# A matrix-memory LSTM with a token and channel mixer: the k q products of two chunks in one run, the transposes in slots 2 and 6

## The chip, the cores and the metric

The kernel runs on one core of a Trainium2 chip. The metric is device time in microseconds (us) of one execution; three executions of the kernel before were timed, at 432.81 us in the median. TensorE is called PE in the profile (PEld for its weight loads), VectorE DVE, ScalarE ACT, GpSimd POOL and SyncE SP; SPq is SyncE's queue, which issues nearly all of the loads here.

## The reference

Four batches of 8 heads, 768 tokens, head width 40. First comes a recurrence with exponential gates, then a token mixer and a channel mixer over the 320 columns of all heads.

```python
for t in range(S):                                   # S = 768
    m_new = np.maximum(f[t] + m, i[t])
    f_stab, i_stab = np.exp(f[t] + m - m_new), np.exp(i[t] - m_new)
    C = f_stab * C + i_stab * outer(v[t], k[t])      # 40 x 40 for each head
    n = f_stab * n + i_stab * k[t]
    y[t] = sigmoid(o[t]) * (C @ q[t]) / max(abs(n @ q[t]), 1)
h  = relu(y.T @ w_tok1) @ w_tok2                     # 768 -> 256 -> 768, over tokens
u  = y + h.T
out = u + relu(u @ w_ch1) @ w_ch2                    # 320 -> 1536 -> 320
```

## The kernel before

**Attention.** Each batch is cut into 6 chunks of 128 tokens; a unit `u` is the pair (batch, chunk), both counted from 0 in the code. In this document the batches are called first to fourth, and chunks go by their number in the code, 0 to 5. In a chunk the recurrence becomes matrix products. `st_s` (L302) multiplies k by q for all 8 heads: 16 matmuls, two at a time on different rows of the array (heads 0 to 3 lie on partitions 0 to 39, heads 4 to 7 on 64 to 103 of the tile `raw`, padded to 64 rows each), and writes two PSUM banks, the tiles `ps_sc`. `st_p` (L312) has VectorE multiply these banks by the decay mask `dd`, one instruction for each bank. `st_state` (L357) adds the chunk to the state: the three products `pu` of k and v, then five VectorE instructions that build the new state `Cn`; for the second batch it also starts the output bank `po` with q times the state before the chunk (L367). `st_pv` (L411) adds the product of masked scores and v to that output. The third and fourth batches (`three(u)`) use `st_pv3` (L388) in its place: the scores are split into three bf16 parts by VectorE (`prep_p2`, `prep_p3`), the product is made from these, q times the state stands behind it (L403), and `st_state` is called at its end.

**Order.** All engines run in program order, as the code is written. `att(b)` (L513) is a generator with five steps a chunk: (1) `st_s` with `st_p`, and loads for the chunk after next; (2) `st_state` or `prep_p3`; (3) the mask's exponentials for the next chunk; (4) `st_pv`, and what follows from its output (`st_hs`, `st_x`); (5) the rest of the next chunk's preparation. The loop at the end (L993) walks 18 slots a batch. A slot holds `gemm1` of one piece of the channel mixer (16 matmuls, L756), then what `more` lists for the slot, then some steps of the next batch's attention, then `gemm2` of the piece before (12 matmuls, L675, in two halves). So the second batch's attention runs inside the first batch's slots 11 to 17 (`STEPS0`, L928), the third's inside the second's slots, and the fourth's inside the third's (`STEPS`, L929). The fourth batch's slots have no attention beside them.

**The slots of the later batches.** `phase_b` (L699) is the second product of the token mixer for one chunk, `phase_t` (L726) transposes the result (three matmuls against the identity, one ScalarE copy and two or three VectorE instructions) so that `gemm1` can read it. In the second to fourth batch the dictionary `more` (L991) puts `phase_b` of chunk 4 into slot 1, `phase_t` of chunk 2 into slot 2, `phase_t` of chunk 3 into slot 4, `phase_b` of chunk 5 into slot 5, and `phase_t` of chunks 4 and 5 into slot 9.

**Banks and loads.** Four PSUM pools of two banks each: `ps_h`, `ps_acc`, `ps_s` (tag "s": the scores, and what is passed `ss`) and `ps_m` (tag "m": outputs, states). A new tile of a pool takes the bank of the tile two before it, and its first writer waits until that tile's last reader is through. The tile `raw` has three buffers, used in turn; its two halves are loaded for the chunk after next, the first in step 1 and the second in step 3 (L228). All loads go out on one queue in the order of the program: for each chunk of the second batch the mask rows `dd` (512 KB), the two halves of `raw` (160 KB each), `q3t` and `pq` (180 KB each) and `kvt` (324 KB), and the gate `sig` (480 KB) twice a batch.

Of the kernel before, what the change touches and what calls it, by code (L numbers as in the profile page):

```python
# [7 lines left out]
F32 = mybir.dt.float32  # L8
# [12 lines left out]
E1 = D + 1  # L21
# [13 lines left out]
def kernel(ctx: ExitStack, tc: tile.TileContext, gates, qk, q3, kv, og,  # L35
# [8 lines left out]
    ps_s = ctx.enter_context(tc.tile_pool(name="ps_s", bufs=2, space=PSUM))  # L44
    ps_m = ctx.enter_context(tc.tile_pool(name="ps_m", bufs=2, space=PSUM))
# [6 lines left out]
    def load_sig(b, i):  # L52
        t = ap.tile([128, NC // 2, DM], F32, tag="sig", name="sig", bufs=3)
        nc.sync.dma_start(out=t, in_=og[b].rearrange("(c p) e -> p c e", p=128)[:, 3 * i:3 * i + 3, :])
        sig[(b, i)] = t
# [111 lines left out]
    def top(x):  # L167
        return x.bitcast(BF16).rearrange("... (t i) -> ... t i", i=2)[..., 1]
# [47 lines left out]
    def sigmoid(b, r=range(2), part=slice(0, 3)):  # L216
        for i in r:
            t = sig[(b, i)][:, part]
            nc.scalar.activation(t, t, AF.Sigmoid)
# [25 lines left out]
    def load_q3(u):  # L245
        b, c = u
        if c > 0:
            load_pq(u, load_q3t(u))
# [53 lines left out]
    def st_s(u, mult=True, mid=iter(()), rows=64, pool=(ps_s, "s")):  # L302
        t = T[u]
        t["s"] = [pool[0].tile([128, 4, L], F32, tag=pool[1], name="ps_sc") for _ in range(2)]
        for h in range(4):
            for hf in range(2):
                r = t["raw"][64 * hf:64 * hf + rows]
                nc.tensor.matmul(t["s"][hf][:, h, :], r[:, 1, h, :], r[:, 0, h, :], start=True, stop=True)  # L308
        if mult:
            st_p(u, mid)  # L310

    def st_p(u, mid=iter(())):  # L312
        t = T[u]
        for hf in range(2):
            if hf:
                next(mid, None)
            dd = t["dd"][:, 4 * hf:4 * hf + 4, :]
            nc.vector.tensor_tensor(dd, t["s"][hf], dd, ALU.mult)  # L318

    def three(u):  # L320
        return u[0] > 1

    def prep_p2(u):
        t = T[u]
        dd = t["dd"]
        r = ap.tile([128, H, L], F32, tag="p12", name="r", bufs=1)
        p3 = xpool[1].tile([128, H, L], BF16, tag="p3", name="p3", bufs=1)
        t["p"] = (top(dd), top(r), p3)
        for hf in range(2):
            h = slice(4 * hf, 4 * hf + 4)  # L330
            nc.vector.tensor_tensor(r[:, h], dd[:, h], top(dd)[:, h], ALU.subtract)
        t["r"] = r
# [24 lines left out]
    def st_state(u, pool=(ps_m, "m")):  # L357
        b, c = u
        t = T[u]
        vx = t["kv"][:, DM:]  # L360
        if c > 0 and not three(u):
            x = int(b == 0)
            t["bank"] = pof = ps_m.tile([128, 512], F32, tag="m", name="po")
            po = pof[:, 0:(x + H) * E1].rearrange("p (h e) -> p h e", e=E1)
            for g, (h0, n) in enumerate(GR):
                y = x if g == 0 else 0
                nc.tensor.matmul(pof[:, (h0 + x - y) * E1:(h0 + x + n) * E1], t["q3"][0][0:n * D, g, :],  # L367
                                 Cst[b][0:n * D, (PG[g] * 3 - y) * E1:(PG[g] * 3 + n) * E1], start=g == 0, stop=False)
            t["po"] = po
        if c < NC - 1:  # L370
            pu = pool[0].tile([120, 3, G3], F32, tag=pool[1], name="pu")
            puf = pu.rearrange("p g e -> p (g e)")
            kwf = t["kw"].rearrange("p h d -> p (h d)")
            for g, (h0, n) in enumerate(GR):
                nc.tensor.matmul(pu[0:n * D, PG[g], 0:n * E1], kwf[:, h0 * D:(h0 + n) * D],  # L375
                                 vx[:, h0 * E1:(h0 + n) * E1], start=True, stop=True)
            cn = ap.tile([120, 3 * G3], F32, tag="C", name="Cn")
            cm = cn if c == 0 else puf
            for (p, a, z) in ((120, 0, 2 * G3), (80, 2 * G3, 2 * G3 + 2 * E1)):
                nc.vector.tensor_tensor(cm[0:p, a:z], puf[0:p, a:z], bm_t[0:p, a:z], ALU.mult)  # L380
            if c > 0:
                for g, (h0, n) in enumerate(GR):
                    sl = (slice(0, n * D), slice(PG[g] * G3, PG[g] * G3 + n * E1))
                    nc.vector.scalar_tensor_tensor(cn[sl], Cst[b][sl], t["decay"][0:n * D, g:g + 1], cm[sl],
                                                   op0=ALU.mult, op1=ALU.add)
            Cst[b] = cn

    def st_pv3(u):  # L388
        b, c = u
        t = T[u]  # L390
        p, w = t["p"], t["v"].rearrange("p j (h e) -> p h j e", h=H)
        ht = ap.tile([128, H, E1], F32, tag="ht", name="ht", bufs=1)
        parts = [(h0, h1, ps_m.tile([128, h1 - h0, 2, E1], F32, tag="m", name="po")) for h0, h1 in ((0, 6), (6, 8))]
        for h0, h1, po in parts:
            for h in range(h0, h1):
                for i, j0, j1 in ((0, 0, 2), (1, 0, 2), (0, 2, 3), (2, 0, 1)):
                    nc.tensor.matmul(po[:, h - h0, 0:j1 - j0], p[i][:, ROW[h], :], w[:, h, j0:j1],  # L397
                                     start=h == h0 and i + j0 == 0,
                                     stop=c == 0 and h == h1 - 1 and i == 2)
        for h0, h1, po in parts if c else ():  # L400
            for g, (g0, n) in enumerate(GR):
                if h0 <= g0 < h1:
                    nc.tensor.matmul(po[:, g0 - h0:g0 - h0 + n, 0], t["q3"][0][0:n * D, g, :],  # L403
                                     Cst[b][0:n * D, PG[g] * G3:PG[g] * G3 + n * E1], start=False, stop=g > 0)
        for h0, h1, po in parts:
            nc.scalar.activation(ht[:, h0:h1], po[:, :, 0], AF.Copy)
            nc.vector.tensor_tensor(ht[:, h0:h1], po[:, :, 1], ht[:, h0:h1], ALU.add)  # L407
        t["ht"] = ht
        st_state(u, (ps_s, "s"))

    def st_pv(u, copy=True):  # L411
        b, c = u
# [96 lines left out]
    def after(u, n):  # L509
        i = units.index(u) + n  # L510
        return units[i] if i < len(units) else None

    def att(b):  # L513
        for c in range(NC):
            u = (b, c)
            n1, n2 = after(u, 1), after(u, 2)
            th = three(u)
            if b + 1 < B and c in (3, 4):
                load_sig(b + 1, c - 3)
            if b > 1 and c == 0:  # L520
                sigmoid(b)
            st_s(u)
            if n2 and not three(u):
                load_phi(n2)
            if n1 and not three(u):
                prep_mask(n1)
            if n2:
                load_qk(n2, 0)
            if th:
                prep_p2(u)  # L530
            yield
            if th:
                prep_p3(u)
            else:
                st_state(u)
            if n1 and three(u):
                prep_mask(n1)
            yield
            if n1:
                prep_exp(n1, 0)  # L540
                if not three(n1):
                    prep_q3(n1)
                    prep_kw(n1)
            if n2:
                load_qk(n2, 1)
                if not th:
                    load_q3(n2)
            yield
            st_pv(u)
            st_hs(u)  # L550
            if not th:
                st_x(u)
            yield
            if n1 and three(n1):
                prep_v(n1)
            if th:
                st_x(u)
            if n1:
                if three(n1):
                    prep_q3(n1)  # L560
                    prep_kw(n1)
                prep_exp(n1, 1)
            if n2:
                load_kv(n2)
                if th:
                    load_q3(n2)
                    load_phi(n2)
            yield
# [244 lines left out]
    t = ps_m.tile([128, HP], F32, tag="m", name="gw")  # L813
# [48 lines left out]
    for c in range(1, NC):  # L862
        u, n1, n2, n3 = (units[c + i] for i in range(4))
# [56 lines left out]
    ss = (ps_s, "s")  # L920
# [10 lines left out]
    for b in range(B):  # L931
# [30 lines left out]
        else:  # L962
# [25 lines left out]
            add_x(b, 5, t5)  # L988
            dec_hi()
            slots = [(k, p) for p in range(6) for k in range(2)] + [(2, p) for p in range(6)]  # L990
        more = {1: [(phase_b, 4, ss)], 2: [(phase_t, 2, ss)], 4: [(phase_t, 3, ss)], 5: [(phase_b, 5)],  # L991
                9: [(phase_t, 4), (phase_t, 5, ss)]}
        for n, (k, p) in enumerate(slots):  # L993
            if b == 0 and 2 < n < 11:
                step(dec_ops(9), 9)
# [101 lines left out]
```

## Time and profile before

| | |
|---|---|
| three executions | 432.74, 432.81, 434.31 us; median 432.81 |
| the profiled execution | 433.07 us |
| its span, first to last instruction | 431.3 us, so 1.8 us lie around it |
| granted TensorE clock, mean over the span | 0.999 |
| PE busy / PEld / DVE / ACT / POOL | 425.4 / 408.0 / 291.9 / 185.3 / 141.7 us |
| matmuls | 3705 |
| share of the chain of waits that is PE | 90% |

How to read it: the time of a stretch of PE is read from the starts of its instructions, since they overlap (a matmul of 0.28 us is followed by the next one after 0.12 us). The timeline prints equal instructions that follow one another as one row, with the count behind; the first number is the start, the second the time until the end of the last.

### The profile page before, as it was taken

The page shows a single profiled execution, that of the slowest core. Times are in us where ns is not written, and L with a number is a line of the kernel's source. Part 1 is how long each engine was busy: PE and PEld are TensorE (multiplying, and loading weights), DVE is VectorE, ACT ScalarE, POOL GpSimd, SP SyncE. Part 2 cuts the span into 40 slices and gives each one's busy share as a digit, 9 for nine tenths or more (in the row PEclk, how much of TensorE's full clock was granted, in tenths as well). Part 3 has the DMA queues.
Part 4 walks back from the last instruction along what each step waited for, and adds up shares of the span by engine and source line. Part 5 has one row for each costly group of instructions (what it writes and reads, how often), then busy time and mean ns, then how long its engine had stood idle before and what let it go on. Part 6 is the DMA issues. An engine that isn't in the chain of part 4 may idle for free.

```text
span 431.3 us, 9405 instructions
## 1 busy us (share of the span) xinstructions
PE 425.4 (99%) x3705; PEld 408.0 (95%) x3706; DVE 291.9 (68%) x656; ACT 185.3 (43%) x426; POOL 141.7 (33%) x186
## 2 busy tenths in 40 slices
PE   8999999999999999999999999999999999999996
PEld 4788999999999999999999999999999999999996
DVE  8999877745777788688795688687885645323212
ACT  6877666894544725324414336234334112211111
POOL 7487485860553410341330330332340110000000
PEclk9999999999999999999999999999999999999999
DMA  7988849903877612145356111343240000000000
GB/s 203 278 264 250 270 142 309 291 27 112 225 218 234 204 56 81 67 130 151 96 168 195 59 64 36 125 130 100 94 115 30 2 17 15 2 32 0 27 7 30
DMA packets 24576, 52.37 MB, mean 121 GB/s; under 512 B 2565, under 2 KB 13325, under 8 KB 24533
## 3 DMA queue, kind: packets, MB, share of 16 engines
q1 hardware_dynamic: 24293, 51.61, 38.8%
q8 instruction: 29, 0.48, 0.5%
q10 hardware_dynamic: 240, 0.18, 0.2%
q14 instruction: 14, 0.11, 0.1%
HBM read 47.73 MB, written 4.04 MB: 120 GB/s over the span
## 4 chain that ended last, share of the span: by engine, by line
PE 90%; DMA 4%; DVE 2%; POOL 2%; ACT 1%; issue 1%; ACTq 0%; SPq 0%; POOLq 0%; DVEq 0%
PE ps_h L756 32%; PE acc L675 30%; PE ps_a L675 5%; PE ps_sc L308 5%; PE ps_b L675 5%; PE po L426 4%; PE po L397 3%; PE pu L375 3%; PE po L403 2%; DMA sig<-in_og_dram 2%; DMA id_t<-in_ident_dram 1%; PE po L367 1%; DMA q3t<-in_q_dram 1%; PE ps_t L737 1%; PE ps_t L735 1%
## 5 line engine op out<-in xcount | busy, mean ns | idle before, releaser
L756 PE MATMUL ps_h<-uT,c1h 128*128 128x256 f32 x720 | 137.8, 283 | 0.2
L761 ACT ACTIVATE gh<-ps_h 128x512 fp32r<-128x512 f32 x72 | 43.0, 597 | 177.8 <-PE ps_h L756 177.5
L756 PEld LDWEIGHTS ps_h<-uT,c1h 128*128 128x128 f32 x720 | 114.0, 188 | 1.4 <-DVE uT L739 0.6
L762 DVE SCALAR_TENSOR_TENSOR gl<-ps_h,gh 128x512 fp32r<-128x512 f32 x72 | 49.6, 689 | 91.6 <-ACT gh L761 91.5
L756 PE MATMUL ps_h<-uT,c1l 128*128 128x256 f32 x432 | 108.5, 281 | 0.0
L675 PE MATMUL acc<-c2h,gh 128*128 128x320 f32 x288 | 90.1, 320 | 0.0
L675 PE MATMUL acc<-c2l,gh 128*128 128x320 f32 x288 | 86.7, 309 | 0.0
L756 PEld LDWEIGHTS ps_h<-uT,c1l 128*128 128x128 f32 x432 | 79.7, 188 | 0.3 <-POOL c1l L669 0.3
L675 PE MATMUL acc<-c2h,gl 128*128 128x320 f32 x288 | 65.6, 309 | 0.0
L675 PEld LDWEIGHTS acc<-c2h,gh 128*128 128x128 f32 x288 | 54.1, 188 | 1.6
L675 PEld LDWEIGHTS acc<-c2l,gh 128*128 128x128 f32 x288 | 54.2, 188 | 0.0
L675 PEld LDWEIGHTS acc<-c2h,gl 128*128 128x128 f32 x288 | 48.1, 188 | 0.3 <-DVE gl L762 0.3
L289 ACT ACTIVATE dd<-dd,bcol 128x128 f32<-128x128 f32 x144 | 45.8, 392 | 3.7 <-POOL dd L279 3.5
L445 POOL TENSOR_TENSOR sig<-sig,ht 128x320 f32<-128x320 f32 x18 | 14.6, 814 | 94.7 <-DVE ht L407 87.7
L496 POOL TENSOR_TENSOR xl<-x,xh 128x320 fp32r<-128x320 f32 x18 | 15.8, 878 | 55.4 <-DVE xh L494 54.0
L318 DVE TENSOR_TENSOR dd<-ps_sc,dd 128x512 f32<-128x512 f32 x48 | 30.8, 680 | 1.9 <-PE ps_sc L308 1.9
L308 PE MATMUL ps_sc<-raw 64*128 64x128 f32 (+1 forms) x384 | 28.0, 285 | 0.0
L308 PEld LDWEIGHTS ps_sc<-raw 64*128 64x128 f32 (+1 forms) x384 | 23.4, 187 | 4.1 <-issue 1.9
L279 POOL TENSOR_SCALAR_AFFINE_SELECT dd<-dd 128x1024 f32<-128x1024 f32 x18 | 21.7, 1208 | 10.2 <-DMA dd<-phi_d 10.2
L426 PE MATMUL po<-kvt,dd 128*128 128x41 f32 (+1 forms) x192 | 23.2, 277 | 0.0
L426 PEld LDWEIGHTS po<-kvt,dd 128*128 128x128 f32 x192 | 22.4, 192 | 0.1
L653 DVE SCALAR_TENSOR_TENSOR pf<-pf,wst 128x384 int32<-128x384 int32 x30 | 16.2, 559 | 6.9 <-POOL wst L633 3.4
(147 smaller groups left out, 750.9 us busy)
## 6 DMA issues: line engine op xcount, KB each, us to landing
dd<-phi_d SPq DMA_DIRECT2D x18, 512.0 KB
wst<-in_wc_dram SPq DMA_DIRECT2D x22, 384.0 KB
kvt<-in_kv_dram SPq DMA_DIRECT2D x24, 324.0 KB
raw<-in_qk_dram SPq DMA_DIRECT2D x48, 160.0 KB
sig<-in_og_dram SPq DMA_DIRECT2D x8, 480.0 KB
out_dram<-x SPq DMA_DIRECT2D x24, 160.0 KB
q3t<-in_q_dram SPq DMA_DIRECT2D x20, 180.0 KB
wst<-in_wt_dram SPq DMA_DIRECT2D x8, 384.0 KB
```

The lines of the kernel that those rows point to most:

```text
L279: nc.gpsimd.affine_select(dd, dd, pattern=[[0, H], [1, L]], compare_op=ALU.is_ge, fill=-1e30, base=0, channel_multiplier=-1)
L289: nc.scalar.activation(dd[:, h, :], dd[:, h, :], AF.Exp, bias=bcol[:, c, HP * b + h:HP * b + h + 1])
L308: nc.tensor.matmul(t["s"][hf][:, h, :], r[:, 1, h, :], r[:, 0, h, :], start=True, stop=True)
L318: nc.vector.tensor_tensor(dd, t["s"][hf], dd, ALU.mult)
L426: nc.tensor.matmul(o, t["dd"][:, ROW[h], :], x, start=c == 0 and h == 0, stop=h == H - 1)
L445: nc.gpsimd.tensor_tensor(sg, sg, ht[:, :, 0:D], ALU.mult)
L496: nc.gpsimd.tensor_tensor(xl, x, f32(xh), ALU.subtract)
L653: v.scalar_tensor_tensor(fi, fi, 3, raw[:, :, 0], op0=ALU.logical_shift_left, op1=ALU.bitwise_or)
L675: nc.tensor.matmul(ps, a, m, start=(first and i == 0), stop=(last and i == n - 1))
L756: nc.tensor.matmul(ps[:, j, :], c1[x][:, a:a + 128], u[:, y, :], start=part is first and i == 0 and (order == 0 or j == 0), stop=i == len( ...
L761: nc.scalar.activation(gh, ps, AF.Relu)
L762: nc.vector.scalar_tensor_tensor(gl, ps, 0.0, f32(gh), op0=ALU.max, op1=ALU.subtract)
```

## The change

The k q products of two neighbouring chunks are issued one behind the other: chunks 2 and 3, and 4 and 5, of the second batch; chunks 1 and 2, and 3 and 4, of the third and fourth. The first chunk of such a pair is called joined. The second chunk's scores go to the two banks of `ps_m`; VectorE's multiplications stay in their steps. In return, the output and state banks of a joined chunk come from `ps_s`. In the third and fourth batch the state update of a joined chunk moves from the end of `st_pv3` to step 2, ahead of it (so that L403 reads the state after the chunk). And in `more`, `phase_t` of chunk 3 moves from slot 4 to slot 2, `phase_t` of chunks 4 and 5 from slot 9 to slot 6, and `phase_b` of chunk 5 writes a bank of `ps_s`.

```diff
+    def joined(u):
+        return u[0] > 0 and u[1] in ((2, 4) if u[0] == 1 else (1, 3))
+
+    def banks(u):
+        return (ps_s, "s") if joined(u) else (ps_m, "m")
...
-            t["bank"] = pof = ps_m.tile([128, 512], F32, tag="m", name="po")
+            t["bank"] = pof = pool[0].tile([128, 512], F32, tag=pool[1], name="po")
...
-        parts = [(h0, h1, ps_m.tile([128, h1 - h0, 2, E1], F32, tag="m", name="po")) for h0, h1 in ((0, 6), (6, 8))]
+        pool, tag = banks(u)
+        parts = [(h0, h1, pool.tile([128, h1 - h0, 2, E1], F32, tag=tag, name="po")) for h0, h1 in ((0, 6), (6, 8))]
...
-        st_state(u, (ps_s, "s"))
+        if not joined(u):
+            st_state(u, (ps_s, "s"))
...
-            st_s(u)
+            if not joined((b, c - 1)):
+                st_s(u, mult=False)
+            if joined(u):
+                st_s(n1, mult=False, pool=(ps_m, "m"))
+            st_p(u)
...
-            else:
-                st_state(u)
+            if not th or joined(u):
+                st_state(u, banks(u))
...
-        more = {1: [(phase_b, 4, ss)], 2: [(phase_t, 2, ss)], 4: [(phase_t, 3, ss)], 5: [(phase_b, 5)],
-                9: [(phase_t, 4), (phase_t, 5, ss)]}
+        more = {1: [(phase_b, 4, ss)], 2: [(phase_t, 2, ss), (phase_t, 3, ss)], 5: [(phase_b, 5, ss)],
+                6: [(phase_t, 4), (phase_t, 5, ss)]}
```

## Rows read from the trace of the kernel before

**Rows 1.** The page: busy time of each engine, share of the span, instructions.

```profile
PE 425.4 (99%) x3705; PEld 408.0 (95%) x3706; DVE 291.9 (68%) x656; ACT 185.3 (43%) x426; POOL 141.7 (33%) x186
```

**Rows 2.** Timeline of PE around one k q run: start, us, engine, line, tiles, count.

```profile
175.24 0.52 PE L756 MATMUL ps_h<-uT,c1h 128*128 128x256 f32 x3
175.59 0.27 PE L756 MATMUL ps_h<-uT,c1l 128*128 128x256 f32 x1
175.79 1.16 PE L308 MATMUL ps_sc<-raw 64*128 64x128 f32 x16
176.88 0.42 PE L675 MATMUL acc<-c2h,gh 128*128 128x320 f32 x1
177.14 0.31 PE L675 MATMUL acc<-c2l,gh 128*128 128x320 f32 x1
177.29 0.31 PE L675 MATMUL acc<-c2h,gh 128*128 128x320 f32 x1
```

**Rows 3.** Timeline of the same run's weight loads.

```profile
175.79 0.97 PEld L308 LDWEIGHTS ps_sc<-raw 64*128 64x128 f32 x16
```

**Rows 4.** Groups by line and shape: count, busy us, mean ns, idle before.

```profile
L308 PEld LDWEIGHTS ps_sc<-raw 64*128 64x128 f32 x368 | 22.4, 187 | 4.0 <-issue 1.9 <-DVE pf L653 0.5 <-DVE Cn L384 0.3
```

**Rows 5.** Timeline of PE, one `phase_t` alone, with the matmuls about it.

```profile
171.61 0.28 PE L756 MATMUL ps_h<-uT,c1l 128*128 128x256 f32 x1
...
172.21 0.31 PE L675 MATMUL acc<-c2l,gh 128*128 128x320 f32 x1
```

**Rows 6.** Timeline of PE, two `phase_t` in a row.

```profile
207.30 0.28 PE L756 MATMUL ps_h<-uT,c1l 128*128 128x256 f32 x1
...
208.23 0.31 PE L675 MATMUL acc<-c2l,gh 128*128 128x320 f32 x1
```

**Rows 7.** Timeline of PE, second batch: runs, first gemm2 matmul behind the output, first output matmul.

```profile
116.91 1.16 PE L308 MATMUL ps_sc<-raw 64*128 64x128 f32 x16
...
123.86 0.39 PE L675 MATMUL acc<-c2h,gh 128*128 128x320 f32 x1
...
128.01 0.80 PE L367 MATMUL po<-Cn,q3t 120*128 120x123 f32 x6
...
132.04 1.16 PE L308 MATMUL ps_sc<-raw 64*128 64x128 f32 x16
...
139.86 0.39 PE L675 MATMUL acc<-c2h,gh 128*128 128x320 f32 x1
...
144.00 0.79 PE L367 MATMUL po<-Cn,q3t 120*128 120x123 f32 x6
```

**Rows 8.** Timeline of SyncE's queue: loads of `raw`, at their issue.

```profile
111.23 0.32 SPq L228 DMA_DIRECT2D raw<-in_qk_dram  x1
...
117.03 0.30 SPq L228 DMA_DIRECT2D raw<-in_qk_dram  x1
...
125.91 0.39 SPq L228 DMA_DIRECT2D raw<-in_qk_dram  x1
...
134.79 0.30 SPq L228 DMA_DIRECT2D raw<-in_qk_dram  x1
...
196.84 0.39 SPq L228 DMA_DIRECT2D raw<-in_qk_dram  x1
```

**Rows 9.** Waits of SyncE's queue, 116 to 118 us: who waited for what, us.

```profile
SPq L228 <- DMA dd<-phi_d: 0.5, 1, 0.5
SPq L253 <- DMA raw<-in_qk_dram: 0.4, 1, 0.4
```

**Rows 10.** The same view, 133 to 136 us.

```profile
SPq L228 <- DMA raw<-in_qk_dram: 0.4, 1, 0.4
```

**Rows 11.** Timeline of VectorE: `st_p` of chunks 3 and 5, second batch, and chunk 1, third.

```profile
126.82 1.28 DVE L318 TENSOR_TENSOR dd<-ps_sc,dd 128x512 f32<-128x512 f32 x2
...
142.59 1.28 DVE L318 TENSOR_TENSOR dd<-ps_sc,dd 128x512 f32<-128x512 f32 x2
...
177.14 1.28 DVE L318 TENSOR_TENSOR dd<-ps_sc,dd 128x512 f32<-128x512 f32 x2
```

## The prediction, made before the changed kernel was built or run

> **What bounds the kernel now.** I read the page's busy times first, then the timeline of PE at the places that the change touches, then the queues that feed these places: VectorE's timeline, and SyncE's with its waits. PE is busy for 99% of the span [rows 1], and between 100 and 350 us its rows follow each other almost without a hole: the time is the length of PE's instruction stream. So the change can gain only what it takes out of that stream, and every wait that it puts in is paid in full. No matmul is added or removed; what is left is what a run costs at its edges, and waits.
>
> **Edges of a k q run.** From the last gemm1 matmul ahead of the run to the second gemm2 matmul behind it 177.14 - 175.59 = 1.55 us pass [rows 2]. Without the run these would be one gemm1 step ((175.59 - 175.24) / 3 = 0.117) and one gemm2 step (177.29 - 177.14 = 0.15), so a run costs 1.55 - 0.12 - 0.15 = 1.29. Inside it, the 16 weight loads take 0.97 us, one 0.187, and they go in pairs: 7 steps in 0.97 - 0.187, 0.112 each [rows 3, 4], so 8 pairs are 0.89. A run that follows another pays 0.89, and 0.395 is saved. There are six joins, two a batch: -2.37 us in all. This is the only gain.
>
> The row shows 0.395 of edge in a run on half the array's rows. The Trainium skill says, in TensorEngine Tiling (Array Packing), Key Properties, that a change of the tiling mode drains the engine; TensorE: Matmul & The Clock Gate, Single matmul latency, puts a drain at about 175 ns. Two drains would be an estimate of 0.35 a run and -2.1 for six; the row is taken.
>
> **Transposes.** One `phase_t` costs 172.21 - 171.61 - 0.27 = 0.33 [rows 5], two in a row 208.23 - 207.30 - 0.27 = 0.66 [rows 6]. Twice 0.33 is 0.66: these runs have no edge to save. Moving them is worth 0 (bounds -0.02 to +0.02 a batch). Cover: chunk 5's `phase_b` now stands one slot ahead of its `phase_t`, with a gemm2 and a gemm1 between (about 1.8 and 1.9 us, 12 x 0.15 and 16 x 0.117) for VectorE's addition and copy; if that cover went, PE would wait for them.
>
> **What the second batch pays: loads.** Chunk 3's products now start right behind chunk 2's, at 116.91 + 0.89 = 117.80 [rows 7], where they stood two slots later. Their data is `raw`, whose second half is issued at 111.23 [rows 8]. When does it land? At 117.03 SyncE gets through a wait for the mask load `dd`, issued just ahead of chunk 3's `raw`, and behind the issue at 117.03 (0.30 long) the next load waits another 0.4 us for a load of `raw` [rows 8, 9]: the first half lands at 117.7, 0.7 behind `dd`. The second lands behind it, at the latest where its run stood before, half a gemm2 (6 x 0.15) behind 123.86, about 124.8 [rows 7]. I take 1.0 us behind the first half, a little over the 0.7 by which that followed `dd`, the nearest row: 118.7, a wait of 0.9 (bounds 0 and 7).
>
> Chunk 5's second half goes out at 125.91, and at 134.79 the queue gets through a wait of 0.4 us for a load of `raw` [rows 8, 10]: the first half lands then, almost nine microseconds after the second was issued, and the second by the same step at 135.8. The loads stand in a backlog, so these times hardly follow a PE that comes later. By then PE has shifted by 0.89 + 0.9 (chunk 3's run and wait) - 1.29 (the run taken away) + 0.8 (next paragraph) = 1.3: chunk 4's run starts at 132.04 + 1.3 = 133.34 [rows 7], chunk 5's could at 134.23 and waits 1.57 (bounds 0.5, the first half alone, and 6, where its run stood before, about 140.7). A longer wait for chunk 3 takes as much off this one.
>
> The issue and landing rows put the landing six to nine microseconds behind the issue. The Trainium skill's DMA: Bandwidth & Descriptors, Rules for kernel authors, says that two loads to disjoint halves of the partitions serialize, which agrees with the second half's place behind the first; its Latency section gives about 2 us of fixed cost a load, by which both would land in time (first rival).
>
> **What the second batch pays: banks.** Chunk 3's output bank (L367) takes the `ps_m` bank that holds chunk 3's scores, so PE waits for VectorE's first multiplication (L318). Before, L367 started 128.01 - 123.86 = 4.15 after the output of chunk 2 was done [rows 7]; the k q run that goes away makes it 4.15 - 1.29 = 2.86. VectorE gets to the multiplication at 126.82, and half of its 1.28 is over at 127.46, 3.6 after the same point [rows 11], since ahead of it in VectorE's queue stand the five instructions that finish chunk 2's output, and these wait for that output. PE waits 0.8, with 0.05 for the release. For chunk 5: 144.00 - 139.86 - 1.29 = 2.85 against 142.59 + 0.64 - 139.86 = 3.37: 0.6. The state's bank behind it needs the second multiplication, 0.6 later, which L367's six matmuls (0.6) cover. Bounds: 0, if VectorE comes sooner, and 0.6 more each, if both halves are waited for.
>
> Second batch: -0.79 + 0.9 + 0.8 + 1.57 + 0.6 = +3.08.
>
> **Third and fourth batch.** Loads have time: the nearest one, the second half for chunk 4, goes out at 196.84 [rows 8], in slot 7, and is used behind slot 8's gemm1: an output product, a gemm2 and a gemm1 lie between, over 4 us, and only two results' stores stand just ahead of it on the queue. I cost it at 0; with a backlog as above it would be some 4 us a batch. The state update of chunk 1 now stands right behind the two runs, in the same slot, and takes the bank of chunk 1's scores: VectorE's first multiplication ends at 177.14 + 0.64 = 177.78 [rows 11], 1.99 after the run's start; PE gets there after 1.09 + 0.89 = 1.98 [rows 2, 3]. A wait of 0.1 with the release; behind it wait gemm2 and all of the stream. Two state updates a batch change their neighbours. Before shows none at the new place, so it costs between nothing and a run's edge, 0.39, each; they had an edge before as well, so I take 0.13 for both. VectorE's five state instructions move ahead of the split output product, whose L403 now waits for them: a gemm2 and a gemm1, 3.7 us, lie between, and cover it; if they didn't, PE would wait there. A batch comes to -0.79 + 0.1 + 0.13 = -0.56, two to -1.12. The fourth batch's own slots have transposes alone: 0.
>
> **Sum.** -1.12 + 3.08 = +1.96 on the profiled execution's 433.07, which lies 0.26 over the median of the runs shown, 432.81; on that median 434.8 us.
>
> **Rivals.**
> - *The waits for loads don't come* (faster than before): chunk 3's and 5's `raw` is there in time, because the backlog is shorter in other executions than in the profiled one. For it: chunk 3 misses by under a microsecond. Against it: chunk 5 misses by 1.57, and the backlog is the same load after load. Then the second batch is -0.79 + 1.4 = +0.6, the sum -0.5: 432.3.
> - *Nothing waits*: the banks are free too, and only the joins and 0.26 for the moved updates count: -2.37 + 0.26 = -2.1, 430.7. Against it: VectorE's queue is chained to the output of the chunk before.
> - *The third and fourth batches wait too* (slower still): PE reaches chunk 1's state bank within 0.01 us of VectorE's multiplication, so any delay of VectorE there is paid at once, twice. For it: slot 2 now gives VectorE a second transpose's instructions just before. Against it: a gemm2 and a gemm1, 3.7 us, lie between. One more multiplication, 0.64 a batch, makes 436.1; from 0.1 us a batch on, the time is over the bound below.
> - *The change doesn't do what it says*: a second run pays its edges again, as it writes other banks. Then +2.37: 437.2. Against it: nothing changes in the shape of the matmuls.
>
> **How the numbers follow.** About 0.5%, 2.2 us, is what a measurement of this kernel can tell from no change: faster is under 430.65, slower over 434.97. The forecast has 0.58, with its own range 433.8 to 435.9, and 0.24 of that lies over 434.97. The rivals have 0.15, 0.06, 0.15 and 0.06. Slower: 0.24 + 0.15 + 0.06 = 0.45. Faster: half of the second rival, 0.03. The rest, 0.52, is within the bound: a loss that is just too small. The range 432.0 to 436.4 leaves out nothing-waits, the last rival and the tails of the other two, 0.2 in all.
>
> **What would show it.** After: two L308 rows of 16, or one of 32, with the second lot 0.89 long in the third and fourth batch; holes on PE ahead of the second lot in the second batch, put down to the load of `raw`, about 0.9 and 1.6 us; holes of 0.8 and 0.6 ahead of L367, put down to L318; a hole of 0.1 ahead of L375 in chunk 1 of the later batches. The prediction is wrong if the L308 rows of chunks 3 and 5 start with no hole, or if PE's stream has grown or shrunk anywhere else by over half a microsecond.

## The result, and the profile after

The changed kernel takes 435.77 us in the median of 12 runs (434.15 to 437.45), the kernel before 433.08 in 12 runs on the same chip (432.73 to 435.35): a ratio of **1.0055 [1.0039, 1.0071]** (in brackets, here and below, the 95% interval). The change makes the kernel 0.55% slower. The profiled execution has a span of 434.6 us and took 436.31; the numbers of the trace below are of this one execution. The granted clock is 1.000 in the mean of this span. Line numbers behind L322 have moved: L367 is now L373, L375 is L381, L403 is L410, L426 is L434, L675 is L687, L756 is L768; L308 and L318 are where they were.

PE's busy time on the page, the chain of waits by engine and line, and the group of the k q products; [rows 1] answers to the first line:

```profile
PE 424.6 (98%) x3705; PEld 408.1 (94%) x3706; DVE 294.9 (68%) x656; ACT 185.3 (43%) x426; POOL 141.6 (33%) x186
...
PE ps_h L768 29%; PE acc L687 28%; PE ps_a L687 5%; PE ps_b L687 5%; PE ps_sc L308 4%; DMA raw<-in_qk_dram 4%; PE po L404 3%; DMA wst<-in_wt_dram 3%; PE po L434 2%; PE pu L381 2%; PE po L410 2%; PE warm L800 1%; PE po L373 1%; DVE pf L665 1%; SPq L228 1%
...
L308 PE MATMUL ps_sc<-raw 64*128 64x128 f32 (+1 forms) x384 | 28.2, 283 | 2.8 <-DMA raw<-in_qk_dram 1.7
```

PE has the same 3705 matmuls and is busy for 0.8 us less, yet the span is 3.3 us longer: the time went into holes. A load of `raw` is on the chain now, and the products of L308 stand idle 2.8 us. Where PE waits in the second batch, 110 to 150 us (who waited for what: us, times, longest; before has no such row in this batch):

```profile
PE ps_sc L308 <- DMA raw<-in_qk_dram: 1.7, 3, 0.7
PE po L373 <- DVE dd L318: 1.1, 2, 0.6
PE ps_sc L308 <- DVE xh L502: 1.0, 1, 1.0
```

The third row is a load as well. VectorE's `xh` is only what ended last by the view; the record of the first half's load ends at 118.69, that of the second at 119.83, and the two rows of L308 that wait start 0.13 behind each. That the loads are moved ahead, and nothing else, takes this row away too (the run with early loads, below).

PE at these places (start, us, engine, line, tiles, count, idle before and its releaser), first the joined runs of the second batch and what follows, answering to [rows 7]:

```profile
116.66 1.16 PE L308 MATMUL ps_sc<-raw 64*128 64x128 f32 x16
118.82 0.46 PE L308 MATMUL ps_sc<-raw 64*128 64x128 f32 x2 [1.00 <-DVE xh L502]
119.96 1.13 PE L308 MATMUL ps_sc<-raw 64*128 64x128 f32 x14 [0.68 <-DMA raw<-in_qk_dram]
121.02 0.39 PE L768 MATMUL ps_h<-uT,c1h 128*128 128x256 f32 x1
...
127.84 0.28 PE L768 MATMUL ps_h<-uT,c1h 128*128 128x256 f32 x1
...
130.44 0.87 PE L373 MATMUL po<-Cn,q3t 120*128 120x123 f32 x6 [0.56 <-DVE dd L318]
...
134.59 1.16 PE L308 MATMUL ps_sc<-raw 64*128 64x128 f32 x16
136.13 0.46 PE L308 MATMUL ps_sc<-raw 64*128 64x128 f32 x2 [0.38 <-DMA raw<-in_qk_dram]
137.23 1.13 PE L308 MATMUL ps_sc<-raw 64*128 64x128 f32 x14 [0.64 <-DMA raw<-in_qk_dram]
138.29 0.42 PE L687 MATMUL acc<-c2h,gh 128*128 128x320 f32 x1
...
146.00 0.28 PE L768 MATMUL ps_h<-uT,c1h 128*128 128x256 f32 x1
...
148.60 0.87 PE L373 MATMUL po<-Cn,q3t 120*128 120x123 f32 x6 [0.56 <-DVE dd L318]
```

Holes are measured from start to start, since a busy row's end is modelled. Two runs joined without a wait take 1.99 (next fence). The first one here takes 121.02 - 116.66 = 4.36, a load wait of 2.37; the second 3.70, a wait of 1.71. The 16 gemm1 matmuls ahead of L373 take 2.60 twice, 0.71 more than the 1.89 of the same group where no wait follows: two bank waits.

The same view in the third batch, two joins; [rows 2] answers to them:

```profile
180.76 2.06 PE L308 MATMUL ps_sc<-raw 64*128 64x128 f32 x32
182.89 0.80 PE L381 MATMUL pu<-kvt,kw 128*120 128x123 f32 x6
...
207.60 2.06 PE L308 MATMUL ps_sc<-raw 64*128 64x128 f32 x32
209.59 0.42 PE L687 MATMUL acc<-c2h,gh 128*128 128x320 f32 x1
```

One row of 32 with no hole: 1.99 for both runs. The 1.09 of a run alone and 0.90 for the second, as predicted from the weight loads. Ahead of the state update it is 2.13, here and in the fourth batch: 0.14 more, where the wait for chunk 1's bank was expected. The view of waits has no row for it, but VectorE's first multiplication there is half done at 182.75 (182.11 and half of 1.28), 0.14 ahead of L381.

VectorE's first multiplications of chunks 3 and 5 ([rows 11] before):

```profile
129.61 1.28 DVE L318 TENSOR_TENSOR dd<-ps_sc,dd 128x512 f32<-128x512 f32 x2
...
147.77 1.28 DVE L318 TENSOR_TENSOR dd<-ps_sc,dd 128x512 f32<-128x512 f32 x2
```

Half of each is done at 130.25 and 148.41; L373 starts 0.19 behind either.

### The profile page after: what moved, and what is told of

It reads as the page before. It is cut to its first block, busy times and chain, and to the rows that moved or that the text cites. A ratio compares the mean times of both kernels' runs of the same rounds, so it can differ in the third digit from the quotient of the medians.

```text
span 434.6 us, 9415 instructions
## 1 busy us (share of the span) xinstructions
PE 424.6 (98%) x3705; PEld 408.1 (94%) x3706; DVE 294.9 (68%) x656; ACT 185.3 (43%) x426; POOL 141.6 (33%) x186
## 4 chain that ended last, share of the span: by engine, by line
PE 83%; DMA 6%; DVE 3%; ACT 3%; issue 2%; SPq 2%; POOL 0%; ACTq 0%; DVEq 0%; POOLq 0%
PE ps_h L768 29%; PE acc L687 28%; PE ps_a L687 5%; PE ps_b L687 5%; PE ps_sc L308 4%; DMA raw<-in_qk_dram 4%; PE po L404 3%; DMA wst<-in_wt_dram 3%; PE po L434 2%; PE pu L381 2%; PE po L410 2%; PE warm L800 1%; PE po L373 1%; DVE pf L665 1%; SPq L228 1%
## 5 line engine op out<-in xcount | busy, mean ns | idle before, releaser
L768 PE MATMUL ps_h<-uT,c1h 128*128 128x256 f32 x720 | 137.6, 282 | 0.2
L768 PEld LDWEIGHTS ps_h<-uT,c1h 128*128 128x128 f32 x720 | 114.0, 188 | 1.1 <-DVE uT L751 0.6
L768 PE MATMUL ps_h<-uT,c1l 128*128 128x256 f32 x432 | 108.2, 281 | 0.0
L687 PE MATMUL acc<-c2h,gh 128*128 128x320 f32 x288 | 89.7, 319 | 0.0
L687 PE MATMUL acc<-c2l,gh 128*128 128x320 f32 x288 | 86.7, 309 | 0.0
L768 PEld LDWEIGHTS ps_h<-uT,c1l 128*128 128x128 f32 x432 | 79.6, 188 | 0.1
L687 PE MATMUL acc<-c2h,gl 128*128 128x320 f32 x288 | 65.6, 309 | 0.1
L687 PEld LDWEIGHTS acc<-c2h,gh 128*128 128x128 f32 x288 | 54.1, 188 | 0.8
L687 PEld LDWEIGHTS acc<-c2l,gh 128*128 128x128 f32 x288 | 54.2, 188 | 0.0
L687 PEld LDWEIGHTS acc<-c2h,gl 128*128 128x128 f32 x288 | 48.1, 188 | 0.3 <-DVE gl L774 0.3
L318 DVE TENSOR_TENSOR dd<-ps_sc,dd 128x512 f32<-128x512 f32 x48 | 30.9, 681 | 1.9 <-PE ps_sc L308 1.9
L308 PE MATMUL ps_sc<-raw 64*128 64x128 f32 (+1 forms) x384 | 28.2, 283 | 2.8 <-DMA raw<-in_qk_dram 1.7
L308 PEld LDWEIGHTS ps_sc<-raw 64*128 64x128 f32 (+1 forms) x384 | 23.9, 187 | 6.7 <-issue 2.7
L434 PE MATMUL po<-kvt,dd 128*128 128x41 f32 (+1 forms) x192 | 23.2, 277 | 0.0
L337 DVE TENSOR_TENSOR r<-dd 128x512 f32<-128x512 f32 x24 | 23.2, 1004 | 0.0
L434 PEld LDWEIGHTS po<-kvt,dd 128*128 128x128 f32 x192 | 22.4, 192 | 0.1
```

The costliest lines, as they stand in the source:

```text
L434: nc.tensor.matmul(o, t["dd"][:, ROW[h], :], x, start=c == 0 and h == 0, stop=h == H - 1)
L687: nc.tensor.matmul(ps, a, m, start=(first and i == 0), stop=(last and i == n - 1))
L768: nc.tensor.matmul(ps[:, j, :], c1[x][:, a:a + 128], u[:, y, :], start=part is first and i == 0 and (order == 0 or j == 0), stop=i == len( ...
```

## The experiments

Each was timed in five rounds beside the kernel before on the same chip; the differences in us are of medians, and the ratios are those of all rounds.

| edit, from the changed kernel | ratio to before | us |
|---|---|---|
| (the change itself) | 1.0055 [1.0039, 1.0071] | +2.7 |
| no joins: transposes and bank of chunk 5's `phase_b` | 1.0066 [1.0054, 1.0078] | +3.1 |
| no joins: transposes alone | 1.0004 [0.9990, 1.0018] | 0.0 |
| joins of the third and fourth batch alone | 0.9976 [0.9965, 0.9987] | -1.1 |
| the same, again | 0.9971 [0.9960, 0.9983] | -1.6 |
| joins of the second batch alone | 1.0094 [1.0075, 1.0113] | +3.7 |
| early loads of `raw` | 1.0000 [0.9988, 1.0012] | 0.0 |
| other banks for chunks 3 and 5 | 1.0042 [1.0025, 1.0058] | +1.8 |
| early loads and other banks | 0.9968 [0.9956, 0.9980] | -1.2 |
| the same program again (`b == 1` for `not th`) | 0.9960 [0.9944, 0.9976] | -1.7 |
| kernel before with early loads | 1.0013 [0.9998, 1.0028] | +0.4 |

**The second part of the change by itself.**

```diff
     def joined(u):
-        return u[0] > 0 and u[1] in ((2, 4) if u[0] == 1 else (1, 3))
+        return False
```

> Only the second part of the change: no chunk is joined, the transposes stand in slots 2 and 6 and chunk 5's second token product writes a bank of the scores' pool. Theory: a run of transposes has no edges, so nothing is saved and nothing waits: within 0.2 us of the kernel before. Rival (the move of the transposes has a part in the loss, since VectorE gets two evacuations in one slot): up to 1 us slower than before.

It was 0.66% slower, a miss. PE in the third batch, the run of chunk 2:

```profile
188.73 0.48 PE L308 MATMUL ps_sc<-raw 64*128 64x128 f32 x2
190.16 1.16 PE L308 MATMUL ps_sc<-raw 64*128 64x128 f32 x14 [0.95 <-DVE x L726]
191.25 0.42 PE L687 MATMUL acc<-c2h,gh 128*128 128x320 f32 x1
```

The run takes 2.52 where it takes 1.09 alone, and the fourth batch has the same hole at 289.56: 2 x 1.43 = 2.9 us of the 3.1. Chunk 5's `phase_b`, just ahead, now writes a `ps_s` bank, and a run needs both of them, so PE waits until VectorE's addition (L726 in this kernel) has read it; the next run puts this to the test. With the joins no run stands there. So this line of the change belongs to the joins, and the edit had not isolated the transposes.

**The transposes alone.** The edit above, and the old bank for chunk 5's `phase_b`:

```diff
-        ... 5: [(phase_b, 5, ss)],
+        ... 5: [(phase_b, 5)],
```

> No joins; the transposes in slots 2 and 6 alone, with phase_b of chunk 5 in its old bank. Theory: 0 within 0.3 us (ratio 0.9993 to 1.0007), the bank of phase_b was what cost 2.9 us in the run that moved it as well. Rival (the place of the transposes itself costs): +0.7 us or more, up to the 2.9, ratio 1.0016 or above, and L308 runs of the later batches still held by VectorE.

The medians agree to 0.01 us, and the run that was held takes its 1.09 again:

```profile
188.35 1.16 PE L308 MATMUL ps_sc<-raw 64*128 64x128 f32 x16
189.44 0.42 PE L687 MATMUL acc<-c2h,gh 128*128 128x320 f32 x1
```

The place of the transposes costs nothing that this comparison can tell.

**Joins of the later two batches alone.**

```diff
-        return u[0] > 0 and u[1] in ((2, 4) if u[0] == 1 else (1, 3))
+        return u[0] > 1 and u[1] in (1, 3)
```

> Chunks joined in the third and fourth batch alone; the second batch as before, transposes as in the changed kernel. Theory (a run's edges cost 0.395 us, the loss is all in the second batch): four joins save 1.58, two waits of 0.14 and the moved state updates give back 0.3 to 0.5, so 1.1 to 1.3 us faster than before. Rival (the edges are paid again in a joined run, or the later batches wait elsewhere): no faster than before, 0 to +0.5.

-0.24% and, on another chip,

> The joins of the later two batches alone, once more, on the chip of the run beside it. Theory: as in its first comparison, 0.9976 within 0.0006, -1.0 us. Rival (its first comparison was a chance): ratio 0.9985 or above.

-0.29%: both intervals are below 1, and both hold the -1.1 us of the prediction's step, a gain of a quarter of a percent. The joined run is one row of 32, as in the changed kernel:

```profile
176.41 2.06 PE L308 MATMUL ps_sc<-raw 64*128 64x128 f32 x32
178.54 0.44 PE L381 MATMUL pu<-kvt,kw 128*120 128x123 f32 x2
```

**Joins of the second batch alone.** Here `joined` is `u[0] == 1 and u[1] in (2, 4)`, with chunk 5's `phase_b` in its old bank.

> The joins of the second batch alone (phase_b of chunk 5 in its old bank, as the later batches aren't joined). Theory: the whole of the change's loss and the 1.07 that the later batches give back on top: after's +2.4 us by medians, plus 1.07, +3.4 us (2.8 to 4.4), ratio 1.0065 to 1.010. Rival (part of the change's loss lies in the later batches or in the moved transposes): +2.4 or less, ratio 1.0055 or below.

+0.94%, 3.7 us by medians. So the parts add up: +3.7 and -1.1 to -1.6 are +2.1 to +2.6, against the change's +2.7. All of the loss, and more than all, is in the second batch.

**Early loads.** Both halves of `raw` are issued at the head of a step, ahead of the other loads. The condition `not th` holds in the first two batches, but `att` is started for the second to fourth alone (`for b in range(1, B)`), and the first batch has its own loop of loads: so the edit reaches the second batch and nothing else.

```diff
+            if n2 and not th:
+                load_qk(n2, 0)
+                load_qk(n2, 1)
...
-            if n2:
+            if n2 and th:
                 load_qk(n2, 0)
...
-            if n2:
+            if n2 and th:
                 load_qk(n2, 1)
```

> The changed kernel, but in the second batch both halves of the k q load are issued at the start of a chunk's first step, ahead of the gate and mask loads, not behind them and in the third step. Theory (PE waits for these loads, 2.4 and 1.7 us in the profiled run of the changed kernel): they land about 1.9 us (a mask load and more) earlier, the first wait falls from 2.4 to under 0.5, the second from 1.7 to under 0.5; what is left is -2.37 for the joins, +1.4 for the banks, +0.5 in the later batches and up to 1 of the load waits: -0.5 to +0.5 against before, 2 to 3 us faster than the changed kernel. Rival (the loads are not what PE waits for, VectorE's multiplications are): the time of the changed kernel, +2.7.

The ratio is 1.0000, inside the theory's range: all of the changed kernel's loss is gone. Of the three waits of the second batch one is left in the same view, the banks':

```profile
PE po L373 <- DVE dd L318: 1.1, 2, 0.6
```

and both runs are one row with no hole:

```profile
117.11 2.06 PE L308 MATMUL ps_sc<-raw 64*128 64x128 f32 x32
119.09 0.38 PE L771 MATMUL ps_h<-uT,c1h 128*128 128x256 f32 x1
...
132.67 2.06 PE L308 MATMUL ps_sc<-raw 64*128 64x128 f32 x32
134.65 0.41 PE L690 MATMUL acc<-c2h,gh 128*128 128x320 f32 x1
```

The control, the same loads in the kernel before:

> The kernel before, with both halves of raw issued at the head of the step in the second batch, and nothing else. Theory (before, no product waits for raw, so an earlier load gains nothing by itself): 0 within 0.4 us, ratio 0.999 to 1.001. Rival 1 (the earlier order is a gain of its own, so that the run with early loads hides a loss that the joins still have): -0.5 us or more, ratio below 0.9988. Rival 2 (the loads that now stand behind raw come late): +0.5 us or more, ratio above 1.0012, and a wait for dd, q3 or kv in the second batch.

+0.13% with an interval that holds 0: no gain of its own. A small cost isn't excluded by the times, but the trace shows none at the place: no wait of PE stands in its second batch, and of the 1.4 us by which its profiled execution is longer, 1.2 have come by the start of chunk 2's run (118.11 where before has 116.91). A hole there,

```profile
77.41 0.41 PE L678 MATMUL acc<-c2h,gh 128*128 128x320 f32 x1 [0.46 <-ACT gh L764]
```

comes 26 us before the first load that the edit moves (103.55), so the edit can't have made it. What the early loads give back is therefore the joins' load wait.

**Other banks for chunks 3 and 5.**

```diff
-        return (ps_s, "s") if joined(u) else (ps_m, "m")
+        return (ps_s, "s") if joined(u) or u[0] == 1 and u[1] > 1 else (ps_m, "m")
```

> The changed kernel, but chunks 3 and 5 of the second batch take their output and state banks from the pool of the joined chunks, not the two banks that hold their own scores. Theory (chunk 5's wait for its load ends at a time that the load queue sets, so what chunk 3 wins is waited for at the load): chunk 3's bank wait of 0.7 falls to 0.2, but the load wait grows by the same; only chunk 5's part is won, 0.2 us: +2.4 to +2.6 against before. Rival (waits add up): both parts are won, 0.7: +2.0. Rival (the banks are the main cause): 1.4 won, +1.3.

+0.42%, +1.8 us: below the theory, between its two rivals, and with an interval (+1.1 to +2.5 us) that reaches all three, so by itself not decisive. The trace is: in the second batch the waits of L373 for VectorE are gone from the view,

```profile
PE ps_sc L308 <- DMA raw<-in_qk_dram: 1.7, 3, 0.8
```

and the holes of the load waits are 0.69 for chunk 3 (the second half was issued at 110.66 and landed at 118.12, here 1.7 us sooner than in the changed kernel's profile) and 2.28 for chunk 5:

```profile
116.63 1.38 PE L308 MATMUL ps_sc<-raw 64*128 64x128 f32 x18
118.26 1.13 PE L308 MATMUL ps_sc<-raw 64*128 64x128 f32 x14 [0.25 <-DMA raw<-in_qk_dram]
...
134.08 0.48 PE L308 MATMUL ps_sc<-raw 64*128 64x128 f32 x2 [0.76 <-DMA raw<-in_qk_dram]
135.28 1.16 PE L308 MATMUL ps_sc<-raw 64*128 64x128 f32 x14 [0.71 <-DMA raw<-in_qk_dram]
```

The time says less about the banks than that, since in this execution the later batches wait too: behind 150 us the view has L404 waiting twice for VectorE's third part of the scores (0.4 us), which the changed kernel's has not.

**Both.** The two edits together:

> The change with both causes of the second batch's loss taken away: both halves of raw are issued at the head of the step, and the outputs of chunks 3 and 5 take the other pair of banks. Theory (the loss is the load waits and the two bank waits, and nothing else): the later two batches keep their -1.07, and the second batch gets its own -0.79, less some 0.2 where the output product still waits a little for VectorE: -1.2 to -1.9 us against before, ratio 0.9955 to 0.9972, and neither the holes ahead of the second 16 products nor the 0.7 us holes ahead of L373 in the trace. Rival (joining the second batch costs something else, or the other banks bring waits of their own): the second batch stays at 0 or above, so -1.1 or less of a gain, ratio 0.9975 or above.

-0.32%, inside the theory's range; and with `b == 1` in place of `not th`:

> The run with early loads and other banks (-0.32% in its comparison), with the early loads in the second batch alone; in that run, and in the two others with early loads, the first batch had them as well. Theory (the second batch's joins, freed of both waits, keep some 0.5 of their 0.79): below the kernel that joins the later batches alone, which stands beside it in this call, by 0.2 to 0.6 us, ratio to before 0.9955 to 0.997. Rival 1 (the second batch's joins are worth nothing even then): equal to that kernel within 0.2, ratio 0.997 to 0.998. Rival 2 (the early loads of the first batch were what helped): worse than -0.32%, ratio above 0.998.

This expectation is wrong on one point: the first batch never had early loads, `b == 1` and `not th` mean the same inside `att`, and both kernels issue the same instructions. So its second rival has nothing to test, and what the run gives is the same program a second time: -0.40% [-0.56, -0.24] beside -0.32% [-0.44, -0.20]. The waits view has no row left between 110 and 150 us in either.

Whether the second batch's two joins, freed of both causes, bring anything shows in the trace and not in the times. The kernel with the four later joins alone, beside it on the same chip, is at -0.29% [-0.40, -0.17]: 0.08 us apart by medians, where the theory had 0.2 to 0.6, and the intervals overlap. In the traces one stretch of PE holds the second batch's joins, with the same matmuls in every version: from the start of chunk 2's run to the start of chunk 5's first output product. Before it is 144.00 - 116.91 = 27.09 [rows 7], and the same within 0.01 in each version that doesn't join the second batch; in the changed kernel 148.60 - 116.66 = 31.94. With both edits, in the second execution:

```profile
117.15 2.06 PE L308 MATMUL ps_sc<-raw 64*128 64x128 f32 x32
...
143.54 0.79 PE L373 MATMUL po<-Cn,q3t 120*128 120x123 f32 x6
```

26.39, and 26.64 in the first (117.64 to 144.28): 0.70 and 0.45 less than before, of the 0.79 that two joins were to save. With the early loads alone it is 27.83, with the other banks alone 29.33. So the two causes are the whole loss of the second batch, and what is left is most of the two joins' gain, in one execution each; the times of whole runs don't resolve it.

## Why the prediction came out as it did

It forecast 434.8 us, a loss just inside what can be told from no change; the kernel is 435.77, a loss just outside it. As a difference, +1.96 was forecast and +2.4 (by the ratio) to +2.7 us (by medians) measured; the rest of the gap is the kernel before, 433.08 here and 432.81 in the forecast. The direction and the mechanism held; one term was too small, and one step came out right by luck.

- **PE's stream is the bound, so every hole is paid.** Held: 1.71 + 2.37 for loads and 1.42 for banks are 5.5 us of holes, -0.79 for the edges of two joins leaves 4.7; less the later batches' 1.1 that is 3.6 against a span that is 3.3 us longer (chunk 2's run starts 0.25 sooner than before, ahead of all joins).
- **Six joins save 0.395 each.** Held by the 1.99 of a joined run ([rows 2] and [rows 3] gave 1.09 + 0.89) and by the later batches alone, -1.1 and -1.6 us against -1.12. (1.55 - 0.12 - 0.15 is 1.28 and not 1.29, which is 0.04 us over six joins. The 0.13 a batch for the moved state updates is inside the -1.12 and wasn't measured by itself.) The page TensorEngine Tiling (Array Packing) of the Trainium skill says under Key Properties that a change of the tiling mode drains the engine. An edge that is paid once for two runs, 1.99 in place of 2 x 1.09 and the edges between, agrees in kind; no run here shows that the edge is a drain.
- **Transposes at 0.** Held, once their bank-mate was kept out of the experiment.
- **Bank waits 0.8 and 0.6.** Measured 0.71 and 0.71. VectorE's order was as read from [rows 11]; the release, put at 0.05, was 0.19.
- **Load waits 0.9 and 1.57.** The term that was mis-sized: 2.37 and 1.71 in the profiled execution. The reading of before was right: in its trace the records of the second halves' loads end at 118.86 and 135.86, where the prediction had 118.7 and 135.8. But these landings were taken as fixed. For chunk 3 the second half was issued at 111.80, 0.57 behind [rows 8], and landed 8.0 us later, at 119.83, 1.1 behind the 118.7 that was taken, while PE came a quarter of a microsecond sooner. Across three executions with the same load order the waits of chunks 3 and 5 are 2.37 and 1.71, 2.16 and 0.93 (the second batch's joins alone), 0.69 and 2.28 (other banks): they vary by over a microsecond each, 3.0 to 4.1 in sum against 2.47 (without the bank waits, PE also comes sooner in the last). The profiled execution lies 0.5 us above its kernel's median.
- **Loads that hardly follow a later PE.** Wrong in the issue, in part wrong in the landing, and hidden by luck. SyncE's queue in the changed kernel, and what it waited for between 110 and 130 us:

```profile
124.73 0.33 SPq L253 DMA_DIRECT2D q3t<-in_q_dram  x1
125.15 0.74 SPq L261 DMA_DIRECT2D pq<-phi_d  x1
127.11 0.36 SPq L242 DMA_DIRECT2D kvt<-in_kv_dram  x1
127.53 0.41 SPq L54 DMA_DIRECT2D sig<-in_og_dram  x1
128.03 0.44 SPq L236 DMA_DIRECT2D dd<-phi_d  x1
128.52 0.83 SPq L228 DMA_DIRECT2D raw<-in_qk_dram  x2
```

```profile
SPq L253 <- PE po L373: 6.0, 1, 6.0
```

The load of `q3t` waits 6.0 us for PE's output product of chunk 2 to free its buffer, and all others queue behind it: it goes out at 124.73 where before had 121.71, and `raw` for chunk 5 is issued the same 3.0 later, since PE's output product came 3.0 later. The landing followed by 1.2 of these (137.09 against 135.86). PE came later too (134.59 against the 133.34 that was worked out), by as much as the landing, so the wait of 1.57 came out at 1.71: two errors of one size. A long wait for chunk 3 did not take as much off chunk 5's.
- **The rivals.** That the loads come in time falls with the holes, and that nothing waits with it. The page DMA: Bandwidth & Descriptors of the Trainium skill, whose section Latency and other measured facts has a fixed cost of about 2 us, stood beside the first; the second halves took 7.4 to 8.2 us from issue to landing in these runs, with other loads ahead, so that cost alone doesn't give the landing here. That the later batches wait falls with 0.14 a batch, predicted 0.1. That a join saves nothing falls with the 1.99.

The issue of chunk 3's `raw` moves by up to 1.5 us between executions (110.66 to 112.15 for the second half) though PE's work ahead of it is the same. SyncE's queue shows where: of the loads ahead of it one takes long to issue. One row from each of four traces, in this order: the changed kernel, before, the second batch's joins alone, the other banks:

```profile
107.04 2.12 SPq L228 DMA_DIRECT2D raw<-in_qk_dram  x1
...
107.72 1.12 SPq L253 DMA_DIRECT2D q3t<-in_q_dram  x1
...
107.93 2.00 SPq L253 DMA_DIRECT2D q3t<-in_q_dram  x1
...
107.44 0.98 SPq L253 DMA_DIRECT2D q3t<-in_q_dram  x1
```

In others, the one with the later joins alone for instance, both take about 0.4. Why one issue takes up to 2 us stays open, and so does why the time from issue to landing varies (last section).

## What to carry to other kernels

Joining two runs on a saturated engine saves their edges, here about 0.4 us a join, and asks for the second run's data and banks earlier; price these two first, at each place by itself, since the same edit gained in two batches and lost more than twice as much in another. A load that lands just in time is to be read with the spread of several executions, and its issue with the whole queue ahead of it: a buffer wait of one load moves all that follow. An experiment on half of a change has to leave out the bank assignments that the other half needs.

## What the runs showed of the hardware

The time from a load's issue to its landing is not fixed by its place in the queue. Chunk 5's second half of `raw` landed 8.2 us behind its issue in the changed kernel (128.93 to 137.09). Issued at the head of the step, ahead of two other loads, it landed 5.5 us behind it with the early loads (125.99 to 131.48) and 7.5 us behind it in the kernel before with the same loads (126.10 to 133.58). The program with both edits had 7.0 in one execution (126.53 to 133.55) and 5.5 in the other (126.04 to 131.54). The issue itself took SyncE 0.3 to 2.1 us for loads of 160 and 180 KB.
